# New planner numbers for the experts' stage: another order, another planned pitch of indirect transfers, three experts allowed to make low halves on TensorE and ScalarE

## The chip, the cores and the metric

The kernel runs on one core of a Trainium2 chip. The metric is the device time of one execution in microseconds (us), as the median of several runs; smaller is better. TensorE is called PE in the profile, its weight loads PEld, VectorE DVE, ScalarE ACT, GpSimd POOL and SyncE SP.

## The reference, cut to what matters

Three blocks follow each other: a linear attention with a delta rule, a dense block with a rational activation, and a block of eight experts to which every token is assigned once.

```python
def _moe2_ref(x, w_gate, w1, w2):          # x 3072 x 384, 8 experts, hidden 1024
    cap = N // E                           # 384 tokens for each expert
    logits = x @ w_gate
    order = np.argsort(-logits.flatten())  # best (token, expert) pairs first
    for idx in order:
        tok, e = (int(idx) // E, int(idx) % E)
        if assigned[tok] >= 0 or counts[e] >= cap: continue
        assigned[tok] = e; counts[e] += 1
    for e in range(E):
        mask = assigned == e
        out[mask] = np.maximum(x[mask] @ w1[e], 0.0) @ w2[e]
```

## The kernel before, in words

The attention and the dense block fill the first 609 us or so; the change does not touch them. The last stage, `tail`, does the eight experts. In each of its rounds one expert fills up (`Route.phase`: VectorE compares keys, TensorE counts with tiny matmuls into `rp`, six rounds of it one after another), which tells the number of the expert whose weights are to be loaded (`ix`) and its 384 tokens (`perm`, three columns of 128 row numbers).

For an expert n the work is this:

- `load` (line 782): two indirect transfers from GpSimd's queue bring `w1f` and `w2f`; `split` makes of each of 16 blocks a half-precision high part on ScalarE (line 793) and the low rest on VectorE (line 794). The parts lie in rings of two, named `w1s`/`w2s` or `wo` in the trace.
- `gather` (line 799): three indirect transfers bring 128 token rows each into `xg`.
- `transp`: TensorE transposes (line 816), ScalarE and VectorE write high and low parts `xe` (lines 819, 820).
- `up`: 8 blocks of 9 matmuls of 384 columns into `eph`, a ring of four (line 828). ScalarE writes the high half of the relu (line 831). The low half has two forms: VectorE computes it in one instruction (line 833), or TensorE subtracts the high half with a matmul by `neg` in the same bank (line 832) and ScalarE writes the relu of what is left (line 834).
- `down`: 3 tiles of 24 matmuls of 384 columns into `px` (line 841), ScalarE to `yo` (line 843), an indirect transfer to the output rows (line 846).

Nothing of this order is written by hand. `Sched` is a list scheduler that runs while the program is built: each piece of work has an engine (or a choice of engines), an assumed duration, the pieces it depends on, a priority (smaller is more urgent) and a latency after its end. At each step it takes the piece that can start first, and among equals the more urgent one. The pieces are then emitted in the order of their planned starts, and each engine works through its own list in that order on the chip, waiting where a semaphore isn't there yet. So the planned durations and the priorities set the order in every queue, GpSimd's of indirect transfers among them, and nothing else.

`PR` holds the priorities of the stage, for each kind of work eight numbers, one for each expert: `cz`, `hu` and `pm` for the routing, `px` transposes, `ev` high halves, `rs` low halves, `up` and `dn` matmuls, `sp`, `sq` and `sl` the weight split, `ga` gathers, `ld` loads, `sc` and `de` the output, `lt` the last matmuls of the dense block. `rp` says for which experts the form on TensorE and ScalarE may be chosen for the low half:

```python
g.add(('ACT',.42,lambda ...: activation(r[:,0,f],P,AF.Relu,scale=1.0-2.0**-11)),[Pn],[(rn,0,f)],pe)
k=g.add(([('PE',.169,lambda ...: matmul(P,s.neg,r[:,0,f],...))] if PR['rp'][n] else [])+
    [('DVE',.484,lambda ...: scalar_tensor_tensor(r[:,1,f],P,0.0,r[:,0,f],op0=OP.max,op1=OP.subtract))],...,ps)
g.add([('ACT',.371,lambda ...: activation(r[:,1,f],P,AF.Relu),lambda on,k=k: on[k]=='PE'),('NOP',0.0,None,...)],...,ps)
```

Of the kernel before, what the change touches and what calls it, by code (L numbers as in the profile page):

```python
# [22 lines left out]
class Att:  # L23
# [149 lines left out]
    def subst(s,m,eng,n16=False,D=None):  # L173
# [17 lines left out]
        if n16: load(None); z.append(lambda: nc.gpsimd.memset(x['W'],0.0))  # L191
# [326 lines left out]
class Ring:  # L518
# [1 line left out]
    def new(s): s.i+=1; return s.cur()  # L520
    def cur(s,d=0): k=(s.i-d)%len(s.t); return s.t[k],(s.name,k)

PR=dict(cz=[-8460.22,-3349.02,-1040.92,-4662.57,2286.09,-4542.55,-2851.07,-2830.4],
    hu=[-1158.71,2769.58,-1952.33,1420.35,20.61,-5092.86,1294.98,-2930.25],
    pm=[-827.35,-3434.29,-7199.64,-301.76,-9380.25,-789.5,-2507.28,-3094.98],
    px=[2213.47,-717.87,711.27,1083.3,-50.99,-1678.84,-176.44,-42.49],
    ev=[-2031.38,3896.44,-445.84,4974.79,-456.6,1410.8,-187.26,-280.73],
    rs=[3995.53,-838.36,3724.15,-2030.4,-5106.28,-2002.19,4963.77,-277.67],
    up=[1432.01,7925.78,415.8,19527.06,1302.29,-2496,-1028.3,393.52],
    dn=[-416.52,-263.26,2914.53,2346.47,7002.88,3039.18,1234.23,2541.59],  # L530
    sp=[-1250.53,-1034.63,-3233.17,3355.56,-2061.84,10814.9,2205.04,145.63],
    sq=[1182.66,5658.8,2518.53,1693.88,5502.59,2521.4,11976.42,-493.54],
    ga=[-91.9,220.07,-1393.31,1453.88,1738,-498.56,-1773.97,252.48],
    ld=[-763.16,-1461.53,2155.57,-1535.71,-2478.81,4661.21,334.89,-1356.37],
    sc=[1792.56,3025.86,-3657.49,-269.42,-11268.81,2802.89,972.48,366.12],
    de=[868.62,405.65,-1417.99,2091.14,378.47,2357.24,-3935.23,-63.01],
    rp=[1,0,0,0,0,0,0,0],
    sl=[9.7,-3928.78,-7440.7,1542.96,-6870.28,-1220,4305.31,-2018.78],
    lt=3989.8,
    tol=0.3)  # L540
class Route:

# [40 lines left out]
    def late(s,ctx): pass  # L583
# [178 lines left out]
class Experts:  # L762
# [16 lines left out]
    def load(s,n,ixn,late=[]):  # L779
        g=s.g; nc=s.nc; ix,ixd=ixn; a,an=s.w1f.new(); b,bn=s.w2f.new()  # L780
        fa=[(an,q) for q in range(8)]; fb=[(bn,q) for q in range(8)]; P1=PR['ld'][n]
        def ld(t,w,sh): return lambda: nc.gpsimd.indirect_dma_start(out=t.rearrange(sh),out_offset=None,in_=w,in_offset=bass.IndirectOffsetOnAxis(ap=ix,axis=0))  # L782
        g.add(('POOL',1.038,ld(a,s.w1,"p g j q -> p (g j q)")),[ixd],fa,P1,post=0.7); g.add(('DMA',4.4,None),fa,fa,0,post=0.9)
        g.add(('POOL',1.038,ld(b,s.w2,"p j f -> p (j f)")),[ixd]+late,fb,P1,post=0.7); g.add(('DMA',4.4,None),fb,fb,0,post=0.9)
        W1,W1n=s.w1s.new(); W2,W2n=s.w2s.new(); s.st.setdefault(n,{}).update(W1=(W1,W1n),W2=(W2,W2n))
        for q in range(16):
            if q<8: x=a[:,q]; W,Wn=W1,W1n; sc=W1S; xn=(an,q)
            else: x=b[:,q-8]; W,Wn=W2,W2n; sc=W2S; xn=(bn,q-8)
            s.split(n,q,x,xn,W[:,0,q%8],W[:,1,q%8],(Wn,0,q%8),(Wn,1,q%8),sc)
    def split(s,n,q,x,xn,h,l,hn,ln,sc):  # L790

        g=s.g; nc=s.nc; p=PR['sp'][n]+PR['sq'][n]*q
        g.add(('ACT',.43,lambda: nc.scalar.activation(h,x,AF.Copy,scale=sc)),[xn],[hn],p)
        g.add(('DVE',.484,lambda: nc.vector.scalar_tensor_tensor(l,x,sc,h,op0=OP.mult,op1=OP.subtract)),[xn,hn],[ln],p+PR['sl'][n])  # L794
    def gather(s,n,pmn):
        g=s.g; nc=s.nc; pm,pmd=pmn; s.st.setdefault(n,{})['pm']=pmn; s.st[n]['x']=s.xe.new()
        for i in range(3):
            t,tn=s.xg.new(); s.st[n]['g',i]=t,tn
            g.add(('POOL',1.038,lambda t=t,i=i: nc.gpsimd.indirect_dma_start(out=t,out_offset=None,in_=s.x2d,in_offset=bass.IndirectOffsetOnAxis(ap=pm[:,i:i+1],axis=0))),[pmd,'x2d'],[tn],PR['ga'][n],post=0.7)  # L799
            g.add(('DMA',.55,None),[tn],[tn],0,post=1.0)  # L800
    def late(s,M,T):

# [9 lines left out]
    def transp(s,n,i):  # L812
        g=s.g; nc=s.nc; xe,xn=s.st[n]['x']; t,tn=s.st[n]['g',i]; sl=slice(128*i,128*i+128); P,Pn=s.ph.new(); P=P.rearrange("p (j t) -> p j t",j=3); p=PR['px'][n]
        gv=t.rearrange("t (p j) -> t j p",j=3)
        def tr():
            for c in range(3): nc.tensor.transpose(P[:,c],gv[:,c],s.ident)  # L816
        k=g.add(('PE',.43,tr),[tn],[Pn],p)
        if (n,i)==(0,0): s.first=k
        g.add(('ACT',.44,lambda: nc.scalar.activation(xe[:,0,:,sl],P,AF.Copy,scale=X2S)),[Pn],[(xn,0,i)],p)  # L819
        g.add(('DVE',.5,lambda: nc.vector.scalar_tensor_tensor(xe[:,1,:,sl],P,X2S,xe[:,0,:,sl],op0=OP.mult,op1=OP.subtract)),[Pn,(xn,0,i)],[(xn,1,i)],p)  # L820
# [14 lines left out]
    def down(s,n):  # L835
        g=s.g; nc=s.nc; W2,W2n=s.st[n]['W2']; pm,pmd=s.st[n]['pm']; r,rn=s.st[n]['r']; pd=PR['dn'][n]; pe=PR['de'][n]
        for i in range(3):
            P,Pn=s.py.new(); o,o_n=s.yo.new()
            for f in range(8):
                for part,(rh,wh) in enumerate(((0,0),(0,1),(1,0))):  # L840
                    g.add(('PE',.17,lambda P=P,rh=rh,wh=wh,f=f,part=part,i=i: nc.tensor.matmul(P,r[:,rh,f,128*i:128*i+128],W2[:,wh,f],start=(f,part)==(0,0),stop=(f,part)==(7,2))),  # L841
                        [(rn,rh,f),(W2n,wh,f)],[Pn],pd+i)
            g.add(('ACT',.42,lambda P=P,o=o: nc.scalar.activation(o,P,AF.Copy,scale=1.0/(X2S*W1S*W2S))),[Pn],[o_n],pe)  # L843
            def out(o=o,i=i):
                nc.gpsimd.memset(s.sp,0.0)
                d=nc.gpsimd.indirect_dma_start(out=s.out,out_offset=bass.IndirectOffsetOnAxis(ap=pm[:,i:i+1],axis=0),in_=o,in_offset=None)  # L846
                for q in s.scat: s.tc.declare_no_dep(d.ins,q.ins,reason="rows of other tokens")
                s.scat.append(d)
            g.add(('POOL',1.08,out),[o_n,pmd],[('sc',o_n)],PR['sc'][n],post=0.7)
            g.add(('DMA',.55,None),[('sc',o_n)],[o_n,('sc',o_n)],0,post=1.0)  # L850
LG=1
def tail(R,X,M,T):
    g=R.g=X.g=Sched(); g.tol=PR['tol']; X.late(M,T)
    R.hurry=PR['hu'][0]; R.cz=PR['cz'][0]; R.pmk=PR['pm'][0]; L={0:R.phase(True)}
    def gather(n): X.gather(n,R.perm(L[n][0],PR['pm'][n]))
    def work(n):
        for i in range(3): X.transp(n,i)
        if n: X.down(n-1)
# [12 lines left out]

def units(g,M,T,u0,xT,newP,NP,O):
# [79 lines left out]
    rs=[-404.57,3136.8,145.19,-3450.88,-1193.48,50.75,4595.25,-486.29,7213.39,-1830.63,672.55,1692.55,767.94,149.92,-4898.99,-833.53],  # L952
    sq=[-4042.56,-4165.8,-3288.62,-1554.54,1129.42,1762.72,-228.16,-1123.11,690.54,4253.9,2705.63,-1743.23,-1487.85,-2504.2,2696.66,553.85],
# [88 lines left out]
class Banks:  # L1042
# [14 lines left out]
    q=[-46.86,-1341.62,713.15,-1006.91,-1360.96],  # L1057
# [50 lines left out]
    rs=-11545.17,  # L1108
    sq=-8925.36,
# [14 lines left out]
    q=1125.43,  # L1124
# [495 lines left out]
```

## Time and profile before

| what | value |
|---|---|
| median of 3 runs | 866.54 us (863.96 to 866.63) |
| the profiled execution's own time | 867.04 us |
| its span, first to last instruction | 865.3 us |
| PE, DVE, ACT, POOL busy | 93%, 85%, 65%, 48% of the span |
| mean granted clock of TensorE | 0.979 of full speed |

The profiled execution lies 0.5 us above the median of the runs. A busy share tells when an engine had an instruction under way; matmuls overlap in the trace, so that a stretch with one matmul after another shows each as about 0.33 us long although a new one starts twice as often. Idle time before an instruction is put down to what released it last.

### The profile page before, as it was taken

The numbers are of one execution on the slowest core, as the hardware profiler recorded it, in microseconds if no ns is written. First come the engines' busy times: TensorE is split into PE (matmuls) and PEld (weight loads), VectorE is DVE, ScalarE is ACT, GpSimd is POOL, SyncE is SP. The second block draws the span as 40 slices with busy tenths as digits, with TensorE's granted clock in tenths as the row PEclk, the third lists the DMA queues.
The fourth block names the chain that finished last, engine by engine and source line by source line (L and its number), as shares of the span: only waits on it lengthen the run. The fifth ranks groups of instructions, "written<-read, shape, count | busy, mean of one in ns | idle before, by whom it ended". The sixth has DMA issues, their size and how long they took to land. (4 is left out here: it accounts for less than half of the span.)

```text
span 865.3 us, 29590 instructions
## 1 busy us (share of the span) xinstructions
PE 808.9 (93%) x12536; PEld 581.0 (67%) x12536; DVE 739.5 (85%) x1696; ACT 563.8 (65%) x1039; POOL 416.8 (48%) x620
## 2 busy tenths in 40 slices
PE   8999789998999999999999999999899899999896
PEld 5887566776677767777777777766556556556563
DVE  8977987888889998998999999996889899889820
ACT  4236767888698787988888889881272451545520
POOL 2256820888678567865786232631221322242501
PEclk9999889999999999999999999999999999999999
DMA  9943387813532524251322201000450542355401
GB/s 362 280 137 84 103 203 211 248 62 75 116 85 81 107 83 97 82 108 31 87 75 67 42 21 39 19 2 20 146 220 29 191 184 112 109 201 229 155 11 45
DMA packets 89588, 98.62 MB, mean 114 GB/s; under 512 B 65776, under 2 KB 73584, under 8 KB 86640
## 3 DMA queue, kind: packets, MB, share of 16 engines
q1 hardware_dynamic: 83072, 59.31, 26.2%
q0 software_dynamic: 6096, 37.23, 11.7%
q8 instruction: 98, 1.61, 0.8%
q14 instruction: 34, 0.28, 0.1%
q10 hardware_dynamic: 288, 0.20, 0.1%
HBM read 74.43 MB, written 17.30 MB: 106 GB/s over the span
## 5 line engine op out<-in xcount | busy, mean ns | idle before, releaser
L936 PEld LDWEIGHTS <-wi 128*128 128x128 f16 x1728 | 168.6, 99 | 38.1 <-issue 6.3
L882 PE MATMUL px<-wo,gg 128*128 128x392 f16 (+1 forms) x1056 | 193.5, 330 | 0.0
L882 PEld LDWEIGHTS <-gg 128*128 128x128 f16 x1056 | 97.8, 98 | 61.8 <-issue 0.7
L900 POOL TENSOR_TENSOR gg<-w,gg 128x512 f16<-128x512 f32 x61 | 71.1, 1166 | 99.6 <-ACT gg L899 92.7
L936 PE MATMUL half<-xT,wi 128*128 128x256 f16 x864 | 107.1, 280 | 3.7 <-DVE wo L1320 2.5
L936 PE MATMUL ph<-xT,wi 128*128 128x256 f16 x864 | 104.2, 275 | 4.5 <-DVE w L913 2.3
L206 POOL TENSOR_TENSOR pmW<-pmW,pmT 128x31 f32<-128x31 f32 (+15 forms) x155 | 89.7, 579 | 10.8
L205 POOL TENSOR_TENSOR pmT<-pmW,pmA 128x31 f32<-128x31 f32 (+15 forms) x155 | 81.3, 525 | 10.9
L841 PEld LDWEIGHTS <-rr 128*128 128x128 f16 x576 | 52.1, 97 | 34.7 <-ACT rr L831 2.8
L846 POOL DMA_INDIRECT out_dram<-yo,perm x24 | 24.3, 1013 | 100.9 <-ACT yo L843 95.5
L831 ACT ACTIVATE rr<-eph 128x384 f16<-128x384 f32 x64 | 30.8, 488 | 59.5 <-PE eph L828 54.4
L899 ACT ACTIVATE gg<-w 128x512 f16<-128x512 f32 x88 | 55.4, 629 | 7.2 <-DVE w L913 6.7
L926 ACT ACTIVATE q<-q 128x512 f32<-128x512 f32 x88 | 54.8, 628 | 4.6 <-DVE q L925 4.5
L841 PE MATMUL px<-wo,rr 128*128 128x384 f16 x288 | 52.7, 330 | 2.4 <-ACT rr L831 2.3
L828 PE MATMUL eph<-xe,w1s 128*128 128x384 f16 x288 | 51.7, 333 | 1.5 <-ACT xe L819 1.0
L841 PE MATMUL px<-w2s,rr 128*128 128x384 f16 x288 | 52.9, 325 | 0.2 <-DVE w2s L794 0.2
L828 PE MATMUL eph<-xe,wo 128*128 128x384 f16 x288 | 51.7, 325 | 0.4 <-ACT xe L819 0.4
L799 POOL DMA_INDIRECT xg<-x2d,perm x24 | 26.4, 1100 | 46.9 <-issue 14.7
L1525 PE MATMUL px<-warm 128*128 128x256 f16 x344 | 44.6, 285 | 2.4 <-DVE warm L1505 2.4
L843 ACT ACTIVATE yo<-px 128x384 f32<-128x384 f32 x24 | 11.5, 490 | 44.9 <-PE px L841 35.7
L828 PEld LDWEIGHTS <-w1s 128*128 128x128 f16 x288 | 26.9, 99 | 19.7 <-issue 3.6
L925 DVE SCALAR_TENSOR_TENSOR q<-q,cf,ph 128x512 f32<-128x512 f32 x44 | 32.4, 737 | 8.7 <-ACT q L919 5.8
(398 smaller groups left out, 1897.6 us busy)
## 6 DMA issues: line engine op xcount, KB each, us to landing
kt<-in_k_dram SPq DMA_DIRECT2D x20, 512.0 KB, 4.5
kn<-in_k_dram SPq DMA_DIRECT2D x12, 384.0 KB, 4.7
qt<-in_q_dram SPq DMA_DIRECT2D x24, 192.0 KB, 3.8
vn<-in_v_dram SPq DMA_DIRECT2D x12, 384.0 KB, 4.4
x2d<-xr SPq DMA_DIRECT2D x44, 96.0 KB, 2.2
xT<-xs SPq DMA_DIRECT2D x22, 144.0 KB, 2.7
wsi<-in_moe_w_in_dram SPq DMA_DIRECT2D x3, 1024.0 KB, 5.4
wst<-in_moe_w_out_dram SPq DMA_DIRECT2D x8, 384.0 KB, 6.2
```

Of the source, the lines that this page charges most:

```text
L205: if half==0: eng.tensor_tensor(t,W[:,0:r,j:j+1].to_broadcast([n,r,k]),A[:,j:j+1,j+1:32].to_broadcast([n,r,k]),op=OP.mult)
L206: else: eng.tensor_tensor(W[:,0:r,j+1:32],W[:,0:r,j+1:32],t,op=OP.subtract)
L828: g.add(('PE',.169,lambda P=P,wh=wh,xh=xh,j=j,f=f,part=part: nc.tensor.matmul(P,W1[:,wh,f,j],xe[:,xh,j],start=(part,j)==(0,0),stop=(part,j ...
L831: g.add(('ACT',.42,lambda P=P,f=f: nc.scalar.activation(r[:,0,f],P,AF.Relu,scale=1.0-2.0**-11)),[Pn],[(rn,0,f)],pe)
L841: g.add(('PE',.17,lambda P=P,rh=rh,wh=wh,f=f,part=part,i=i: nc.tensor.matmul(P,r[:,rh,f,128*i:128*i+128],W2[:,wh,f],start=(f,part)==(0,0), ...
L882: te.matmul(T['px',un//8][bp][:,0:O.N],gg()[:,gh,i,128*bp:128*bp+128],M.wo[:,wh,fb,0:O.N],start=fb==0 and n==0,stop=fb==15 and n==2,skip_g ...
L899: ac.activation(T['gg',un][:,0].rearrange("p f t -> p (f t)")[:,a:b],T['w',un][:,a:b],AF.Copy)
L900: def gl(e): return lambda: e.tensor_tensor(T['gg',un][:,1].rearrange("p f t -> p (f t)")[:,a:b],T['w',un][:,a:b],T['gg',un][:,0].rearrang ...
L925: add(('DVE',.07+.6*z,lambda: ve.scalar_tensor_tensor(q(),q(),cf[:,4:5],P(),op0=OP.add,op1=OP.mult)),Q+Pn,Q,un+O.pd('mu',un))
L926: add(('ACT',.22+.37*z,lambda: ac.activation(q(),q(),AF.Abs)),Q,Q,un+O.pd('f2',un))
L936: for wh,xh in ((0,0),(0,1),(1,0)): te.matmul(T['P',un][:,i],M.wi[:,wh,part,128*fb:128*fb+128],xT()[:,xh,part],start=n==0,stop=n==8); n+=1
L1525: for _ in range(n): nc.tensor.matmul(bk[t or 'px1'][:,0:256],warm[:,0:128],warm,start=True,stop=True)
```

## The change

All of it is in numbers that the planner uses. Every priority of `PR` gets a new value; `rp` goes from one expert to three; an indirect transfer is planned with 1.27 us of GpSimd's time in place of 1.038 us (loads, gathers) or 1.08 us (outputs). No instruction's form, no tile and no other planned duration changes.

```diff
-PR=dict(cz=[-8460.22,-3349.02,-1040.92,-4662.57,2286.09,-4542.55,-2851.07,-2830.4],
...
-    lt=3989.8,
+PR=dict(cz=[-7021.72,-4284.48,1384.12,-7207.49,1083,-12767.81,-1178.86,-1110.34],
...
+    up=[496.03,1660.13,3217.1,3239.03,-324.52,-123.65,-619.57,-4288.44],
+    dn=[1561.31,5887.23,19537.55,-1015.14,85.3,922.9,1565.23,2415.17],
...
-    rp=[1,0,0,0,0,0,0,0],
+    rp=[1,1,1,0,0,0,0,0],
...
+    lt=-4685.38,
...
-        g.add(('POOL',1.038,ld(a,s.w1,"p g j q -> p (g j q)")),[ixd],fa,P1,post=0.7); g.add(('DMA',4.4,None),fa,fa,0,post=0.9)
-        g.add(('POOL',1.038,ld(b,s.w2,"p j f -> p (j f)")),[ixd]+late,fb,P1,post=0.7); g.add(('DMA',4.4,None),fb,fb,0,post=0.9)
+        g.add(('POOL',1.27,ld(a,s.w1,"p g j q -> p (g j q)")),[ixd],fa,P1,post=0.7); g.add(('DMA',4.4,None),fa,fa,0,post=0.9)
+        g.add(('POOL',1.27,ld(b,s.w2,"p j f -> p (j f)")),[ixd]+late,fb,P1,post=0.7); g.add(('DMA',4.4,None),fb,fb,0,post=0.9)
...
-            g.add(('POOL',1.038,lambda t=t,i=i: nc.gpsimd.indirect_dma_start(out=t,out_offset=None,in_=s.x2d,...
+            g.add(('POOL',1.27,lambda t=t,i=i: nc.gpsimd.indirect_dma_start(out=t,out_offset=None,in_=s.x2d,...
...
-            g.add(('POOL',1.08,out),[o_n,pmd],[('sc',o_n)],PR['sc'][n],post=0.7)
+            g.add(('POOL',1.27,out),[o_n,pmd],[('sc',o_n)],PR['sc'][n],post=0.7)
```

## Rows read from the trace of the kernel before

**Rows 1.** Windows: us, busy us and instructions of each engine, PEclk, DMA share, GB/s
```profile
623.50:857.00 233.50, 218.78 (x1676) 134.54 (x1676) 183.66 (x656) 104.01 (x239) 66.04 (x83) 0.99 0.38 140
660.00:745.00 85.00, 77.75 (x631) 48.05 (x630) 76.75 (x289) 36.64 (x85) 24.14 (x30) 0.99 0.41 149
742.70:746.10 3.40, 3.38 (x19) 1.79 (x17) 1.09 (x4) 2.13 (x5) 1.08 (x2) 0.50 0.09 37
```

**Rows 2.** Timeline of TensorE, two stretches: start, us, line, tiles, count, idle before
```profile
785.85 6.17 PE L828 MATMUL eph<-xe,wo 128*128 128x384 f16 x37
...
806.47 0.62 PE L816 MATMUL eph<-ident,xg 128*128 128x128 f32 x3 [1.36 <-DMA xg<-x2d,perm]
...
835.81 9.43 PE L841 MATMUL px<-w2s,rr 128*128 128x384 f16 x57
845.07 11.86 PE L841 MATMUL px<-wo,rr 128*128 128x384 f16 x72
```

**Rows 3.** Waits of TensorE from 623.5 to 857 us: us, times, longest
```profile
PE eph L816 <- DMA xg<-x2d,perm: 5.4, 8, 1.4
PE px L841 <- ACT rr L831: 2.3, 1, 2.3
PE rp L686 <- DVE fl L685: 2.2, 4, 1.2
PE eph L828 <- ACT xe L819: 1.5, 2, 1.0
```

**Rows 4.** Timeline of GpSimd's queue around two gathers: start, us, transfer, idle before
```profile
669.28 0.99 POOL L799 DMA_INDIRECT xg<-x2d,perm  x1 [7.42 <-issue]
670.58 0.96 POOL L799 DMA_INDIRECT xg<-x2d,perm  x1 [0.30 <-issue]
671.84 0.95 POOL L799 DMA_INDIRECT xg<-x2d,perm  x1 [0.30 <-PE rp L675]
673.09 1.18 POOL L782 DMA_INDIRECT w1f<-in_moe_w_dram,ix  x1 [0.30 <-DVE y L690]
674.58 1.20 POOL L782 DMA_INDIRECT w2f<-in_moe_w_dram,ix  x1 [0.31 <-issue]
...
801.38 3.03 POOL L799 DMA_INDIRECT xg<-x2d,perm  x1 [0.30 <-PE rp L751]
804.71 0.94 POOL L782 DMA_INDIRECT w2f<-in_moe_w_dram,ix  x1 [0.30 <-issue]
```

**Rows 5.** The gathers' tile: durations in ns, then us from issue to landing
```profile
L799 POOL DMA_INDIRECT xg<-x2d,perm x24: 945/990/3027, 619.8 to 812.2; - x24
...
DMA to landing us min/median/max: 3.0/3.5/5.7
```

**Rows 6.** Timelines of ScalarE and TensorE at one late weight load
```profile
680.38 1.35 ACT L793 ACTIVATE w1s<-w1f 128x384 f16<-128x384 f32 x3 [3.04 <-DMA w1f<-in_moe_w_dram,ix]
681.64 0.85 ACT L831 ACTIVATE rr<-eph 128x384 f16<-128x384 f32 x2
682.16 0.82 PE L841 MATMUL px<-wo,rr 128*128 128x384 f16 x4 [2.33 <-ACT rr L831]
```

**Rows 7.** Groups by line: xcount | busy, mean ns | idle before, releaser
```profile
L833 DVE SCALAR_TENSOR_TENSOR rr<-eph,rr 128x384 f16<-128x384 f32 x56 | 30.4, 551 | 9.6 <-ACT rr L831 9.5
L832 PE MATMUL eph<-rr,neg 128*128 128x384 f16 x8 | 1.9, 325 | 0.3 <-ACT rr L831 0.3
L834 ACT ACTIVATE rr<-eph 128x384 f16<-128x384 f32 x8 | 3.3, 500 | 0.0
```

**Rows 8.** Waits of TensorE from 660 to 745 us
```profile
PE rp L675 <- DVE cs L677: 1.4, 3, 0.9
PE rp L686 <- DVE fl L685: 0.7, 2, 0.4
PE eph L816 <- DVE rr L833: 0.5, 1, 0.5
PE rp L751 <- DVE pD L749: 0.4, 1, 0.4
```

**Rows 9.** Timeline of VectorE beside the long gather
```profile
801.17 2.42 DVE L794 SCALAR_TENSOR_TENSOR wo<-w1f,wo 128x384 f16<-128x384 f32 x5
```

**Rows 10.** Waits of ScalarE from 590 us on
```profile
ACT w1s L793 <- DMA w1f<-in_moe_w_dram,ix: 13.9, 4, 7.9
```

More of the change, by code (lines that the diff above doesn't have):

```diff
@@ L521, in cur @@
     def cur(s,d=0): k=(s.i-d)%len(s.t); return s.t[k],(s.name,k)
-PR=dict(cz=[-8460.22,-3349.02,-1040.92,-4662.57,2286.09,-4542.55,-2851.07,-2830.4],
[L524 to L536, printed above, removed]
-    rp=[1,0,0,0,0,0,0,0],
-    sl=[9.7,-3928.78,-7440.7,1542.96,-6870.28,-1220,4305.31,-2018.78],
-    lt=3989.8,
@@ new lines @@
+PR=dict(cz=[-7021.72,-4284.48,1384.12,-7207.49,1083,-12767.81,-1178.86,-1110.34],
+    hu=[4367.29,-1095.31,-2497.75,1447.83,-2105.69,-7597.14,1027.7,-2629.82],
+    pm=[-3475.17,1722.28,1057.64,-2113.23,5840.09,-4513.16,-1490.95,-956.24],
+    px=[-137.6,-3474.66,1460.08,448.12,1024.11,-342.1,861.87,-2871.22],
+    ev=[160.92,-3120.26,116.8,2928.69,551.57,543.59,1506.35,3637.96],
+    rs=[-3504.24,-511.95,5358.35,-300.41,-11135.9,-901.21,-336.22,-1754.47],
+    up=[496.03,1660.13,3217.1,3239.03,-324.52,-123.65,-619.57,-4288.44],
+    dn=[1561.31,5887.23,19537.55,-1015.14,85.3,922.9,1565.23,2415.17],
+    sp=[5811.28,5969.32,1234.8,-29.41,-1471.48,825.42,3800.92,4596.91],
+    sq=[681.16,5242.16,3332.63,25311.96,912.45,7313.85,33672.88,1654.22],
+    ga=[-724.27,-3968.76,5224.32,-173.49,3719.71,2350.61,-2575.84,-289.48],
+    ld=[6348.84,-1482.53,4524.46,-3311.1,3863.06,-2234.93,-1983.38,-1522.24],
+    sc=[-604.13,1497.92,-2905.62,6311.2,4227.11,-2931.29,-3523.47,3303.07],
+    de=[-35.98,1416.71,-8044.03,-6322.47,-7301,-4333.83,6190.61,1133.9],
+    rp=[1,1,1,0,0,0,0,0],
+    sl=[5589.05,2182.64,1906.44,223.23,932.54,496.68,3030.77,-666.54],
+    lt=-4685.38,
@@ L798, in gather @@
             t,tn=s.xg.new(); s.st[n]['g',i]=t,tn
-            g.add(('POOL',1.038,lambda t=t,i=i: nc.gpsimd.indirect_dma_start(out=t,out_offset=None,in_=s.x2d,in_offset=bass.IndirectOffsetOnAxis(ap=pm[:,i:i+1],axis=0))),[pmd,'x2d'],[tn],PR['ga'][n],post=0.7)
+            g.add(('POOL',1.27,lambda t=t,i=i: nc.gpsimd.indirect_dma_start(out=t,out_offset=None,in_=s.x2d,in_offset=bass.IndirectOffsetOnAxis(ap=pm[:,i:i+1],axis=0))),[pmd,'x2d'],[tn],PR['ga'][n],post=0.7)
             g.add(('DMA',.55,None),[tn],[tn],0,post=1.0)
```

## The prediction

> **What bounds the kernel now.** I read the windows first, because the change can act in the last stage alone. From the first transposition of gathered rows (623.5 us) to the last matmul (857 us) TensorE is busy for 218.8 of 233.5 us, VectorE for 183.7, ScalarE for 104.0 and GpSimd for 66.0 [rows 1]. TensorE sets the end: in its timeline the last 129 matmuls follow each other without a gap [rows 2], and what comes after 857 us is one output transfer and the end of the program, some 8 us that no order changes. A matmul of 384 columns costs (6.17 - 0.33)/36 = 0.162 us of this queue, not the 0.33 us of its record [rows 2]. So the time of the stage is TensorE's own work plus its idle time, 233.5 - 218.8 = 14.7 us. A new order can only win from those 14.7 us.
>
> The view of waits splits them: 5.4 us for gathered rows in 8 waits, 2.3 us in one wait for a high half, and smaller ones for the routing and the inputs on VectorE and ScalarE [rows 3]. VectorE is the second limit: between 660 and 745 us it is busy for 76.8 of 85 us, while TensorE idles for 85 - 77.75 = 7.25 us [rows 1]. GpSimd is far from full. Its transfers matter by the time at which they start.
>
> **The change part by part.** Every term is taken against the profiled execution's 867.04 us, which is 0.5 us above the median of the runs.
>
> *The pitch of transfers.* In GpSimd's timeline five transfers one behind the other start at 669.28 to 674.58 us, that is 1.33 us apart [rows 4], where the planner counted 1.038. The third gather thus starts 0.5 us later than planned and the load behind the gathers 3.81 - 3 x 1.038 = 0.7 us later. TensorE obeys its list and stands still at the transposition meanwhile. Eight waits of 5.4 us are 0.68 us each, about the size of this error. One of them, 1.36 us [rows 2], belongs to a gather that took 3.03 us instead of 0.99 [rows 4, 5], which no single planned number covers. Of the other 4.0 us I take two thirds as saved, 2.7 us: with 1.27 us the planner puts other matmuls ahead of the transposition. From issue to landing a gather takes 3.5 us [rows 5]; the plan's parts now add up to 1.27 + 0.7 + 0.55 + 1.0 = 3.52 us, before to 3.29. Bounds: nothing to 5.4 us saved.
>
> By the Trainium skill, page "SBUF — State Buffer", section "Who interferes with whom", a VectorE instruction with two inputs in SBUF shuts out a GpSimd instruction that reads SBUF until it is done. The trace agrees at one place: the gather of 3.03 us starts 0.21 us after the start of five weight splits, which run on VectorE for 2.42 us [rows 4, 9]. By the medians the sum below holds; by this rule it would be about 2.7 us higher, since no fixed pitch is right beside splits (a rival below).
>
> *The load behind the gathers.* At 680.38 us ScalarE has stood for 3.04 us before weights that haven't landed; behind it in its queue are two high halves, and for these TensorE waits 2.33 us [rows 6]. The load left 0.7 us late by the working above, so I take 0.7 us saved, bounds nothing to 2.3.
>
> *VectorE's relief.* At most 16 low halves (experts 1 and 2) leave VectorE. In a run each costs it (2.42 - 0.55)/4 = 0.47 us (2.42 us is the run of five splits, 0.55 the length of one record) [rows 7, 9], 7.5 us in all. Where they lie, between 660 and 745 us, TensorE waits for VectorE 1.4 + 0.7 + 0.5 + 0.4 = 3.0 us [rows 8]. I take half, 1.5 us. Bounds: nothing (the routing's chain sets those waits by its own length), 3.0 directly, and 7.5 if each routing round behind them moves forward whole.
>
> *What TensorE and ScalarE take over.* Sixteen matmuls by 0.162 us are 2.6 us on the engine that sets the end. The eight of expert 0 waited 0.3 us once for their high half [rows 7], so sixteen may add 0.6. Half of the 2.6 us should fall into the 7.25 us in which TensorE idles there anyway: cost 1.3 us, bounds nothing to 3.2; extra matmuls can't win time by themselves. A matmul by `neg` waits for ScalarE, and the next `up` matmuls stand behind it. ScalarE gets 16 x 0.50 = 8 us more [rows 7], which I price at nothing, covered by its 129 idle us of 233.5. That cover fails where the relu of a low half stands in ScalarE's queue behind a split whose weights aren't there: ScalarE waited 13.9 us in 4 such waits [rows 10]. Then the `down` matmuls that read the low half are late next, 2.3 us as in rows 6. If the planner finds VectorE free earlier it keeps the old form; then this term and the relief both vanish.
>
> *The clock.* From 742.7 to 746.1 us TensorE ran at a granted clock of 0.50, the lower level of 1.2 GHz [rows 1], just behind gather and routing waits. That costs about 1.7 us. If the waits shrink it may vanish; an order with other waits may have such a stretch elsewhere. I take 0.8 us saved, bounds 1.7 either way.
>
> *The order itself.* All priorities are new, so each queue (TensorE's, VectorE's, ScalarE's, GpSimd's transfers) is shuffled inside the rings. That moves no work off TensorE and is covered by the terms above. SP's queue and the first gather, at 619.8 us [rows 5], are not touched: it waits for rows of the dense block.
>
> Sum: 2.7 + 0.7 + 1.5 - 1.3 + 0.8 = 4.4 us less. 867.04 - 4.4 = 862.6, and with the 0.5 us to the median 862.1, say 862 us. All gains at their direct bounds and no cost give 12.4 us less, about 854; no gain, all costs (3.2), one late low half (2.3) and one more slow stretch (1.7) give 7.2 us more, about 874.
>
> **The rivals.**
> 1. *Low halves late on ScalarE (slower).* For experts 1 and 2 one relu each falls behind a split that waits for weights. Cost 2.6 + 0.6 + 2 x 2.3 = 7.8 us, against 2.7 + 0.7 from the pitch: 4.4 us more, about 871 us. For it: rows 6 and 10 show that very queue blocked. Against it: loads are planned later now, so splits are placed later too. It decides from the point where both experts have such a wait; with one it comes to 2.1 us more.
> 2. *The waits only change places.* TensorE idles for 14.7 us again behind other gathers and routing rounds, and the added matmuls hide in that or cost 1.3: 866.5 to 868 us. For it: a routing round is a chain between VectorE and TensorE [rows 8], whose length no order changes. Against it: 5.4 us of the waits have a cause that the new number removes.
> 3. *The relief passes on whole.* The routing behind experts 1 and 2 comes 7.5 us earlier instead of 1.5: 856 us. For it: VectorE at 90% there [rows 1]. Against it: TensorE would then have to find work for nearly all of its idle time.
> 4. *GpSimd held up by VectorE.* Two more gathers fall beside runs of splits and take 3 us, each with a wait of 1.36 us [rows 2]: 862.1 + 2.7 = 865 us. That is what the skill's page, named above, would lead to. For it: the one gather of rows 5. Against it: the median is 0.99.
>
> **How the numbers follow.** A measurement here tells about 0.3%, 2.6 us, from no change: faster is below 863.9 us, slower above 869.1. Chances: my forecast 0.42, rival 1 0.20, rival 2 0.17, rival 3 0.13, rival 4 0.08. Of my forecast's share 0.03 lies above 863.9. So faster 0.39 + 0.13 = 0.52, same 0.03 + 0.17 + 0.08 = 0.28, slower 0.20. The range of 855 to 870 us takes in all of my forecast, rivals 2 and 4, most of rival 3 and the lower half of rival 1; it leaves out about 0.15. The forecast's own range is 859 to 865 us, the terms at half or one and a half of their values.
>
> **What would show it.** The step on the pitch is right if TensorE's waits for gathered rows fall from 5.4 us to about 3 while GpSimd's pitch stays at 1.3 us. The relief is right if the instructions of line 832 rise from 8 towards 24, those of line 833 fall by as many, and the routing waits between 660 and 745 us halve. The wait at line 841 for a high half should shrink; if one of 2 us or more stands there for ScalarE's line 834, rival 1 is at work. Idle time of TensorE of 14.7 us as before, spread over other lines, is rival 2. A gather of over 2 us beside splits is rival 4. I am wrong as a whole if TensorE's idle time falls and the time does not, or if a stage before 609 us has moved.

## The result, and the profile after

The changed kernel takes 851.98 us, the median of 4 runs (848.24 to 854.94), against 865.25 (860.14 to 866.63) for the kernel before on the same chip: a ratio of 0.9855, with an interval of 0.9809 to 0.9901. The gain is about 13 us where the prediction had 4.4, and the time lies below the range of 855 to 870.

The profiled execution took 853.05 us, its span is 851.3. Not all of the difference of 14 us to the profiled execution before belongs to the change: line 1552, where the experts' stage is set up, starts at 589.71 us in the trace of before and at 587.35 in that of after, although the instructions ahead of it are in the same order on every engine. In the profiles of all kernels of this study, none of which changes this part, line 1552 starts at 585.1 to 593.3 us. From there to the first transposition it is 33.8 us before and 33.4 after. What follows is therefore told in the *stage*, from the start of the first transposition (line 816) to the end of the last matmul (line 841): 623.51 to 856.93 us before, **233.4 us**, and 620.70 to 842.96 after, **222.3 us**, that is 11.2 less. After it come 8.3 us in both (7.0 in the four runs below with transfers of SyncE, whose totals are shorter by these 1.3 us as well).

The windows after: us, busy us and instructions of PE, PEld, DVE, ACT and POOL, granted clock, DMA share, GB/s. The first is the stage, the second the stretch of [rows 1].

```profile
620.70:843.00 222.30, 216.89 (x1685) 134.28 (x1685) 179.48 (x647) 109.10 (x248) 67.28 (x83) 0.99 0.39 147
660.00:745.00 85.00, 82.71 (x717) 52.11 (x715) 79.40 (x320) 43.31 (x99) 27.06 (x33) 1.00 0.42 153
742.70:746.10 3.40, 3.40 (x23) 2.04 (x22) 3.40 (x18) 1.06 (x3) 2.67 (x4) 1.00 0.53 152
624.90:628.40 3.50, 3.50 (x23) 1.81 (x22) 1.97 (x10) 0.49 (x1) 0.00 (x0) 0.51 0.53 225
```

TensorE idles for 222.30 - 216.89 = 5.4 us by this view, 14.7 before, with nine matmuls more. Between 660 and 745 us it idles for 2.3 us instead of 7.25. The stretch of half clock at 742.7 us is gone; one early in the stage, which the kernel before has too, is left. TensorE is busy nearly all through such a stretch of 3.4 us at half the granted clock, so that one costs up to 1.7 us, an estimate from these windows.

The waits of TensorE in the stage, beside [rows 3] (us, times, longest); then from 660 to 745 us, beside [rows 8]:

```profile
PE eph L816 <- DMA xg<-x2d,perm: 3.3, 8, 0.8
PE rp L686 <- DVE fl L685: 0.6, 1, 0.6
PE eph L828 <- ACT xe L819: 0.6, 1, 0.6
PE rp L673 <- DVE ge L617: 0.4, 1, 0.4
PE px L841 <- ACT yo L843: 0.3, 1, 0.3
...
PE eph L816 <- DMA xg<-x2d,perm: 2.0, 4, 0.8
PE px L841 <- ACT yo L843: 0.3, 1, 0.3
```

The wait of 2.3 us for a high half has gone, and so have all waits for VectorE from 660 to 745 us. The gathers, and the groups of the low halves, beside [rows 5] and [rows 7]:

```profile
L799 POOL DMA_INDIRECT xg<-x2d,perm x24: 946/1132/1832, 616.4 to 798.7; - x24
...
DMA to landing us min/median/max: 3.0/3.2/3.8
...
L833 DVE SCALAR_TENSOR_TENSOR rr<-eph,rr 128x384 f16<-128x384 f32 x47 | 25.9, 552 | 8.5 <-ACT rr L831 8.3
L834 ACT ACTIVATE rr<-eph 128x384 f16<-128x384 f32 x17 | 8.0, 494 | 4.4 <-PE eph L832 4.4
L832 PE MATMUL eph<-rr,neg 128*128 128x384 f16 x17 | 5.2, 325 | 0.0
```

TensorE now makes 17 low halves, six for expert 0 and eleven for experts 1 and 2. GpSimd's pitch has not become shorter: from one gather's start to the next's it is 1.39 us by the median, 1.30 before. What changed is what stands around the gathers. GpSimd's timeline where the loads of expert 2 leave, beside [rows 4]:

```profile
663.41 0.99 POOL L782 DMA_INDIRECT w1f<-in_moe_w_dram,ix  x1 [6.47 <-DVE pn L715]
664.70 0.96 POOL L782 DMA_INDIRECT w2f<-in_moe_w_dram,ix  x1 [0.30 <-issue]
672.70 1.09 POOL L799 DMA_INDIRECT xg<-x2d,perm  x1 [7.04 <-PE rp L675]
674.09 1.13 POOL L799 DMA_INDIRECT xg<-x2d,perm  x1 [0.30 <-issue]
```

The loads leave 9.7 us earlier than in [rows 4], 6.9 if one counts from the start of the stage, ahead of the gathers instead of behind them.

### The profile page after: what moved, and what is told of

The parts are those of the page before. It is cut to its first block, busy times and chain, and to the rows that moved or that the text cites. A ratio compares the mean times of both kernels' runs of the same rounds, so it can differ in the third digit from the quotient of the medians.

```text
span 851.3 us, 29600 instructions
## 1 busy us (share of the span) xinstructions
PE 807.2 (95%) x12545; PEld 580.9 (68%) x12545; DVE 735.9 (86%) x1687; ACT 568.9 (67%) x1048; POOL 417.1 (49%) x620
## 3 DMA queue, kind: packets, MB, share of 16 engines
q0 software_dynamic: 6096, 37.23, 11.8%
## 4 chain that ended last, share of the span: by engine, by line
PE 52%; DVE 17%; issue 11%; DMA 7%; POOL 7%; ACT 3%; SPq 1%; POOLq 0%; DVEq 0%; ACTq 0%
PE px L882 13%; PE half L936 8%; PE ph L936 8%; PE eph L828 4%; PE px L841 3%; DMA xg<-x2d,perm 3%; POOL pmW L206 2%; PE px L1525 2%; POOL pmT L205 2%; PE tg L123 2%; PE tg L269 2%; PE px L761 1%; DVE w L913 1%; DMA w1f<-in_moe_w_dram,ix 1%; PE tg L260 1%
## 5 line engine op out<-in xcount | busy, mean ns | idle before, releaser
L846 POOL DMA_INDIRECT out_dram<-yo,perm x24 | 26.7, 1111 | 82.1 <-ACT yo L843 80.2
L1525 PEld LDWEIGHTS <-warm 128*128 128x128 f16 x352 | 33.8, 102 | 9.5 <-DVE warm L1505 2.4
```

The costliest lines, as they stand in the source:

```text
L1525: for _ in range(n): nc.tensor.matmul(bk[t or 'px1'][:,0:256],warm[:,0:128],warm,start=True,stop=True)
```

## The experiments

Each ran beside the kernel before on the same chip; the ratio is to that kernel. The stage comes from one profiled execution each, the ratio from several runs. *Old order* is the kernel before, *new order* the kernel after, with the edit named. A stage from one profile can be off by more than e1 shows: the stretches at half clock early in it last 3.4 us in the kernel after and 6.8 in e14, whose edit acts only later.

| run | edit | ratio, 95% interval | stage, us |
|---|---|---|---|
| before | | 1 | 233.4 |
| after | | 0.9855 [0.9809, 0.9901] | 222.3 |
| e1 | after once more | 0.9872 [0.9832, 0.9911] | 222.8 |
| e2 | old order, 2nd and 3rd gathers off GpSimd's queue | 0.9875 [0.9832, 0.9918] | 223.3 |
| e3 | new order, the same | 0.9818 [0.9781, 0.9856] | 217.3 |
| e4 | new order, 11 low halves back on VectorE | 0.9901 [0.9871, 0.9932] | 226.2 |
| e13 | new order, both | 0.9869 [0.9821, 0.9916] | 222.9 |
| e5 | old order, 16 low halves on TensorE | 1.0087 [1.0052, 1.0122] | 240.2 |
| e6 | old order, expert 2's loads first | 0.9984 [0.9961, 1.0007] | 230.9 |
| e15 | old order, e2 and e6 together | 0.9874 [0.9833, 0.9915] | 226.8 |
| e14 | new order, expert 2's loads last | 1.0067 [1.0039, 1.0095] | 239.2 |
| e16 | new order, e14 and e4 together | 1.0122 [1.0062, 1.0182] | 242.5 |
| e7 | old priorities, planned with 1.27 us | 1.0136 [1.0093, 1.0179] | 241.4 |
| e8 | old priorities, three experts allowed | 1.0049 [1.0027, 1.0072] | 234.7 |
| e9 | other priorities, planned with 1.40 us | 0.9947 [0.9919, 0.9975] | 225.8 |
| e10 | new order, gathers delayed | 0.9912 [0.9885, 0.9938] | 227.9 |
| e11 | e9, gathers delayed | 0.9928 [0.9905, 0.9952] | 229.0 |
| e12 | old order, gathers delayed | 1.0041 [1.0014, 1.0069] | 236.6 |

**e1: the kernel after once more.** No edit; it shows how far the stage repeats.

> The changed kernel once more, to see how well the time of the last stage repeats. By the two profiles that stage (first transposition of gathered rows to last matmul) took 233.4 us before and 222.3 us after, while the stages ahead of it, whose instructions are the same in both kernels, differed by 2.4 us. If the gain lies in the stage, this run shows 222 us there within 1.5 us, whatever the whole time does.

The stage repeats within 0.5 us, the ratio within its interval. Of the 13 us of the first measurement, 11 can be counted on.

**e2, e3: the second and third gather of each expert without GpSimd's queue.** SyncE brings as many bytes of fixed rows instead, so the assignment of tokens is left out for these rows. These transfers do not wait for the routing either: in e2 the two of expert 1 leave at 613.4 and 613.9 us, that expert's first gather at 637.4.

```diff
-lambda t=t,i=i: nc.gpsimd.indirect_dma_start(out=t, ... in_offset=IndirectOffsetOnAxis(ap=pm[:,i:i+1],axis=0))
+lambda t=t,i=i: nc.gpsimd.indirect_dma_start(... as before ...) if i==0 else nc.sync.dma_start(t,s.x2d[128*(3*n+i):128*(3*n+i)+128])
```

> The order of before, with the second and third gather of each expert as plain transfers of SyncE's queue (fixed rows, so which token goes to which expert is left out). That takes 16 transfers of 1.3 us from GpSimd's queue, and no transposition but an expert's first can wait for a late gather. Theory pitch (the old order was planned for gathers that come too soon, and in queues worked through in order each late one holds up other work behind it): the stage falls by 5 us or more, from 233.4 to about 228, with fewer waits on VectorE and ScalarE too. Theory order (the old order is simply worse, and gathers matter only where TensorE waits for them): it falls by about 3 us, the part of the 5.4 us of waits that the second and third gathers have, and the waits for routing steps and high halves stay.

> The same edit in the order of after (again the rows are fixed ones). Theory pitch: the new order already allows for late gathers, so the stage falls by 2 us or less from 222.3. Theory order: it falls like the old order did, by the second and third gathers' part of its 3.3 us of waits, about 2 to 3 us.

The stage falls by 10.1 us in the old order and by 5.0 in the new one. In e2 the theory of the pitch was right on the 5 us or more, but not on fewer waits for VectorE. In e3 both theories missed: 2 to 3 us was the most that either allowed. TensorE's waits in e2 from 620 us on:

```profile
PE eph L816 <- DMA xg<-x2d,perm: 2.3, 3, 1.3
PE rp L686 <- DVE fl L685: 2.2, 6, 0.8
PE rp L675 <- DVE cs L677: 1.7, 4, 1.0
```

Not all of the 10.1 us is shown to be the gathers', because the two stages ran at different clocks. The kernel before has two stretches at half clock in its stage (626.7 and 742.7 us), e2 none, and e3, e4 and e13 have the early one, like the kernel after. The early stretch before, the whole stage of e2, and the early stretches of e4, e13 and e3 (columns as above):

```profile
626.70:630.10 3.40, 3.40 (x17) 1.68 (x17) 1.74 (x7) 0.00 (x0) 0.00 (x0) 0.50 0.83 354
622.97:846.28 223.31, 214.09 (x1676) 133.27 (x1676) 183.49 (x656) 102.91 (x239) 50.47 (x68) 1.00 0.38 143
622.30:625.70 3.40, 3.32 (x21) 1.73 (x21) 1.56 (x5) 0.03 (x1) 0.00 (x0) 0.50 0.77 322
628.50:631.90 3.40, 3.18 (x21) 1.64 (x21) 1.71 (x5) 0.17 (x1) 0.00 (x0) 0.50 0.39 128
626.40:629.80 3.40, 3.08 (x20) 1.58 (x19) 1.80 (x5) 0.27 (x1) 0.00 (x0) 0.51 0.43 133
```

At 1.7 us for a stretch, 3.4 of the 10.1 us are clock, and 6.7 are left. Whether the gathers' waits bring the stretches on is open; e3 and e13 have the same fast gathers as e2 and still the early stretch. The listed wait for gathers fell by 5.4 - 2.3 = 3.1 us in the old order and by 3.3 - 0.8 = 2.5 in the new one, where the number of stretches is the same. So in both orders the stage fell by about twice what the line of waits lost, or more. The waits for VectorE stay: they are not the gathers' doing.

**e4: the low halves of experts 1 and 2 back on VectorE, in the new order**, at the places of the two instructions that they replace. It moves eleven, not the nine of which the expectation speaks.

```diff
-[('PE',.169,lambda ...: matmul(P,s.neg,r[:,0,f],start=False,stop=True))]
+[('PE',.169,(lambda ...: matmul(...)) if n==0 else None)]
-('ACT',.371,lambda ...: activation(r[:,1,f],P,AF.Relu), ...)
+('ACT',.371,(lambda ...: activation(...)) if n==0 else (lambda ...: nc.vector.scalar_tensor_tensor(r[:,1,f],P,0.0,r[:,0,f],op0=OP.max,op1=OP.subtract)), ...)
```

> The order of after, with the nine low halves of expert 1 that it gave to TensorE and ScalarE (17 less expert 0's eight) done by VectorE in the same places. VectorE gets 9 x 0.47 = 4.2 us more and TensorE 9 x 0.16 = 1.5 us less. Theory relief (the freed VectorE makes the gain): the stage takes 3 us or more longer, 225 us or above. Theories pitch and order: between 1.5 us shorter and 1 us longer.

The theory of the relief came true: it costs 226.15 - 222.26 = 3.9 us (3.4 against e1), with one early stretch at half clock in all three, although TensorE has eleven matmuls less, 11 x 0.162 = 1.8 us. VectorE's relief is thus worth 5.2 to 5.7 us gross. TensorE's waits in e4:

```profile
PE rp L673 <- DVE ge L617: 1.3, 1, 1.3
PE eph L828 <- DVE rr L834: 1.0, 1, 1.0
PE rp L739 <- DVE pc L738: 0.9, 1, 0.9
PE rp L710 <- DVE eo L701: 0.6, 1, 0.6
```

Four waits for VectorE that the kernel after does not have add up to 3.8 us, three of them on the routing. The group that VectorE got, with its xcount, busy us and mean ns:

```profile
L834 DVE SCALAR_TENSOR_TENSOR rr<-eph,rr 128x384 f16<-128x384 f32 x11 | 6.0, 549 | 0.0
```

**e13: both edits in the new order.**

```diff
+... if i==0 else nc.sync.dma_start(t,s.x2d[128*(3*n+i):128*(3*n+i)+128])   # gathers, as in e3
+('PE',.169,(lambda ...: matmul(...)) if n==0 else None)                    # low halves, as in e4
```

> The kernel after with two edits together: the second and third gathers of each expert are plain SyncE transfers of fixed rows (the assignment of tokens is left out for those rows), and the low halves of experts 1 to 7 that TensorE and ScalarE make are VectorE's again, at the same places. Alone the first gave a stage of 217.3 us, the second 226.2, the kernel after 222.3. Theory one (separate prices): the low halves cost their 3.7 us again, 220.5 to 221.5. Theory two (VectorE is late only because the gathers are): 217.5 to 218.8, their price is under 1.5.

With the gathers off the queue the low halves cost 222.93 - 217.31 = 5.6 us, more than the 3.9 with them on it and than theory one allowed. Theory two falls: VectorE was not late because the gathers were. And 222.9 is nearly the old order's 223.3: with fast gathers and the low halves on VectorE, the two orders are worth about the same, 0.4 us apart by the stages and 2.1 if the half-clock stretch of e13, which e2 lacks, is taken out. With the low halves on VectorE late gathers cost the new order only 226.15 - 222.93 = 3.2 us, for a line of waits that is 2.6 us shorter.

**e5: the low halves of experts 1 and 2 on TensorE in the old order**, at the places of VectorE's instruction.

```diff
-[('DVE',.484,lambda ...: scalar_tensor_tensor(r[:,1,f],P,0.0,r[:,0,f],op0=OP.max,op1=OP.subtract))]
+[('DVE',.484,(lambda ...: scalar_tensor_tensor(...)) if n not in (1,2) else (lambda P=P,f=f: [matmul(P,s.neg,r[:,0,f],start=False,stop=True),activation(r[:,1,f],P,AF.Relu)]))]
```

> The order of before, with the sixteen low halves of experts 1 and 2 done by TensorE and ScalarE in the places where VectorE did them. VectorE gets 16 x 0.47 = 7.5 us less, TensorE 16 x 0.162 = 2.6 us more. In the order of after the opposite edit on 11 low halves cost 3.6 us of the stage. Theory relief (VectorE's time alone counts): the stage falls by 3 to 5 us from 233.4. Theory pitch (in the old order late gathers set the pace, and VectorE only waits longer when it is freed): it changes by less than 1.5 us either way, or rises by up to 2.6.

Both theories missed: it is slower by 6.7 us of the stage. Of these, 16 x 0.162 = 2.6 us are matmuls, and 6.8 us more at half clock than before make up to 3.4. The ratio over eight executions says 7.5. The waits for routing steps do not get shorter: at lines 675, 686 and 751 TensorE waits 5.5 us for VectorE, 4.0 before. The exchange wins 3.9 us for eleven low halves where the order was made for it and loses 6.7 for sixteen where it was not. Here the matmul and the second relu stand where VectorE's instruction stood, which no planner chose; e8, in which the planner places them under the old priorities, gains nothing either.

**e6, e15: expert 2's loads ahead of its gathers, in the old order.** The planned starts of the `ix` step (line 706, third round) and of the two loads are moved 10 us ahead when the pieces are emitted; in e15 the edit of e2 is there too.

```diff
-for a0,_,f,i in sorted(order,key=lambda x:x[:2]): emit(a0,i,f)
+# key of a piece: its planned start plus s.sh.get(i,0), never below the keys of what it depends on
+for a0,o,f,i in sorted(order,key=lambda x:(key[x[3]],x[1])): emit(a0,i,f)
+g.sh.update({k:-10.0} if n==2 else {})   # at both transfers of load, and at the third ix step
```

> The order of before, with one thing moved: expert 2's index step on VectorE and its two weight loads go ahead of its three gathers, as in the order of after, where the loads left GpSimd 9.7 us sooner. All other queues keep their order. In the profile of before ScalarE stood 3.0 us for these weights and TensorE 2.3 us behind it. If that late load is a part of the gain, the wait of line 841 for a high half goes and the stage falls by 2 us or more; if the late gathers hold that stretch up anyway, less than 1 us, and the gathers of expert 2, now 2.7 us later in their queue, take the place of the wait.

> The kernel before with expert 2's loads ahead of its gathers and the second and third gathers of each expert as plain SyncE transfers of fixed rows (the assignment of tokens is left out for those rows). Alone the first gave a stage of 230.9 us, the second 223.3, the kernel before 233.4. Theory one (separate prices): 220.5 to 221.3. Theory two (the load was late only because it stood behind gathers, so that the two prices are one): 222.5 to 223.8.

In e6 the wait for a high half at line 841 shrinks from 2.3 us to none, and the stage is 2.5 us shorter. But its first transposition comes 1.2 us later behind its gather than before (4.9 us, 3.7 before). From the issue of that gather to the end of the stage the move wins 1.3 us, as much as the total says (0.9984 [0.9961, 1.0007], 1.4 us, not to be told from no change). One half-clock stretch fewer would be enough for that, and other waits open instead, 1.9 us at line 751 for VectorE (0.4 before).

For e15 stage and total disagree: the stage is 3.5 us longer than e2's, the total is e2's. Of the 3.5 us, 3.3 lie at one place, where a first gather takes 5.1 us from its issue to the transposition and a stretch at half clock follows. TensorE waits 2.17 us there, 0.61 in e2, and the stretch is worth up to 1.7:

```profile
793.80 0.81 PE L816 MATMUL eph<-ident,xg 128*128 128x128 f32 x3 [2.17 <-DMA xg<-x2d,perm]
...
794.00:797.40 3.40, 3.40 (x14) 2.26 (x14) 1.63 (x6) 0.98 (x2) 1.60 (x3) 0.51 0.89 355
```

Without these two e15 lies at 223.5 us, which is theory two: as far as one profile tells, the early loads win nothing where the gathers are off the queue. Prices that add up (220.5 to 221.3) do not fit the stage, and the total shows no sign of them.

**e14, e16: expert 2's loads behind its gathers, in the new order**, by the same means (loads 13.5 us later, and the splits behind them); e16 has the edit of e4 too.

```diff
+g.sh.update({k:13.5} if n==2 else {})   # at both transfers of load
```

> The kernel after with the two loads of expert 2 moved on GpSimd's queue from ahead of that expert's three gathers to behind them, as they stand in the kernel before; the splits of these weights follow later. Theory one (the load's place is worth in the new order what it was in the old): the stage goes from 222.3 to 224 to 225.5 and a wait for late splits of expert 2 at the second products comes back. Theory two (the new order has cover for it): under 1 us more.

> The kernel after with the loads of expert 2 behind its gathers and the low halves of experts 1 to 7 all on VectorE. Theory one (the prices are separate and the gathers' places in the order hold the rest): 228 to 229.5 us for the stage, so that some 4 to 5 of the 11 us are left between it and the kernel before. Theory two (low halves and load relieve the same waits): 226 to 227.5. If it comes to 232 or more, these two edits are the whole gain and the gathers' places none of it.

Both theories missed by far: the one edit costs 16.9 us, more than the whole gain. The timelines of GpSimd, ScalarE, VectorE and TensorE in e14 show one chain:

```profile
677.92 0.95 POOL L782 DMA_INDIRECT w1f<-in_moe_w_dram,ix  x1 [0.30 <-issue]
...
684.98 3.41 ACT L793 ACTIVATE w1s<-w1f 128x384 f16<-128x384 f32 x8 [11.42 <-DMA w1f<-in_moe_w_dram,ix]
...
685.53 3.37 DVE L794 SCALAR_TENSOR_TENSOR w1s<-w1f,w1s 128x384 f16<-128x384 f32 x7 [8.96 <-ACT w1s L793]
688.82 0.26 DVE L690 SCALAR_TENSOR_TENSOR y<-y,dd,dg 128x48 bf16<-128x48 bf16 x1
689.12 0.56 DVE L617 TENSOR_TENSOR ge<-y,ramp 128x768 bf16<-128x768 bf16 x1
...
689.73 0.34 PE L673 MATMUL rp<-oh,ge 128*128 128x32 bf16 x6 [11.77 <-DVE ge L617]
```

The load leaves at 677.92 us and ScalarE's split starts 7.1 us later. VectorE's half of the split waits for ScalarE's, and behind it in VectorE's queue stand the steps of the routing for which TensorE's next instruction waits. TensorE, with work for other experts further back in its queue, stands still for 11.8 us. The granted clock falls in this pause and stays low for the first microseconds of the work behind it; the windows of both (columns as above):

```profile
677.60:689.80 12.20, 0.43 (x5) 0.10 (x5) 4.24 (x10) 4.82 (x12) 1.99 (x4) 0.60 0.70 275
689.80:700.10 10.30, 10.30 (x77) 6.33 (x78) 8.45 (x41) 4.99 (x12) 3.05 (x3) 0.81 0.16 44
```

Of the 16.9 us, 11.8 are this one stop; an early stretch of 3.4 us more at half clock and the 3.9 us of half clock behind the stop make up to 3.7 more. With e14 as its base, e16 costs 3.3 us more, again about the price of the low halves. By the expectation of e16, 232 us or more would make the low halves and the load the whole gain. Its 242.5 us do not show that: they lie above the kernel before, so the late load does harm here that it does not do in the old order, and its price is no share of the gain.

**e7, e8: the two new permissions under the old priorities**, each alone, the order planned anew from them.

```diff
-('POOL',1.038, ...   # e7: both loads and the gather, and 1.08 for the output
+('POOL',1.27, ...
-rp=[1,0,0,0,0,0,0,0]  # e8
+rp=[1,1,1,0,0,0,0,0]
```

> The priorities of before, planned with 1.27 us for an indirect transfer, and nothing else. Theory pitch in its plain form (the measured number by itself makes the gain): the stage falls by 4 us or more. Theory search (the priorities are numbers found for one set of durations and mean little under another): the order changes in many places at once and the stage gets longer, 235 us or more, in spite of the truer number.

> The priorities and the pitch of before, with the form on TensorE and ScalarE allowed for three experts, and nothing else. The planner now chooses the form and the order around it moves too. Theory relief: the stage falls by 3 us or more from 233.4. Theory search: no gain, 232 us or more.

Both are slower than before. The theory of the search came true in both. In e7 the waits for gathers do fall, to 1.9 us, but others open. TensorE's waits from 620 us on:

```profile
PE rp L675 <- DVE cs L677: 4.6, 6, 1.3
PE rp L713 <- DVE gs L705: 3.6, 1, 3.6
PE px L841 <- ACT yo L843: 3.6, 3, 1.7
PE eph L816 <- DMA xg<-x2d,perm: 1.9, 3, 1.1
```

A truer number alone wins nothing here, under priorities found for another one.

**e9: other priorities, planned with a pitch of 1.40 us.** Only the numbers of `PR` and the four durations differ from the kernel after.

```diff
-('POOL',1.27, ...
+('POOL',1.4, ...
-PR=dict(cz=[-7021.72, ...],hu=[4367.29, ...], ...)
+PR=dict(cz=[-43976.15, ...],hu=[46543.09, ...], ...)
```

> The kernel after with other priorities for the steps of the expert stage, and with 1.40 in place of 1.27 us for each of the four transfers that GpSimd issues there (the median pitch of neighbours in the kernel after is 1.37 to 1.38 us); nothing else differs. Theory one, that an order pays when transfers come later than it reckoned with: the stage, 222.3 us in the kernel after, comes to 218 to 221 with less waiting for gathers than its 5.4 us, and the total is 0.2 to 0.6% below the kernel after's. Theory two, that the new order gains by its low halves and loads and the pitch is beside the point: any other order is as good or worse, 222 to 226 us.

The waits for gathers fell as expected, from 3.3 to 1.4 us (the line of the kernel after is 3.3, not the 5.4 that the expectation names), but the stage is 3.5 us longer, although it has no stretch at half clock. Other waits come instead, most of them for VectorE's steps. TensorE's waits in e9:

```profile
PE rp L686 <- DVE fl L685: 2.4, 5, 0.8
PE px L841 <- ACT yo L843: 1.9, 2, 1.6
PE rp L675 <- DVE cs L677: 1.8, 5, 0.8
PE eph L816 <- DMA xg<-x2d,perm: 1.4, 2, 1.1
```

VectorE's own group of low halves in e9 is late too (busy us, mean ns, then the idle time before them and what ended it):

```profile
L833 DVE SCALAR_TENSOR_TENSOR rr<-eph,rr 128x384 f16<-128x384 f32 x46 | 25.2, 554 | 15.0 <-ACT rr L831 14.8
```

VectorE stands for 14.8 us in front of low halves whose high halves ScalarE has not made (8.3 after). So it looks as if room for the gathers was bought with VectorE's order, which no run tests alone. Theory one holds for the gathers and fails for the stage, which lies in the range of theory two.

**e10, e11, e12: a memset of GpSimd ahead of each gather** (0.41 us each), in the new order, in that of e9 and in the old one.

```diff
-lambda t=t,i=i: nc.gpsimd.indirect_dma_start(...)
+lambda t=t,i=i: [nc.gpsimd.memset(s.sp,0.0),nc.gpsimd.indirect_dma_start(...)]   # s.sp is 1 x 384
```

> The kernel after with a GpSimd memset of 384 numbers on one partition ahead of each of its 24 gathers, so that neighbours come some 0.2 to 0.4 us further apart; the order is the same. Theory one (an order tolerates the pitch that it was made for and loses beyond it): the stage grows by 3 us or more, from 222.3 to 225 to 230, all of it in waits of the transpositions for gathers and in what these pass on. Theory two (the gathers' pitch is beside the point): it grows by less than 1 us.

> The order for 1.40 us with the same memset ahead of each gather. Theory one: it has some room left, so that it loses about half of what the kernel after loses by the same delay, 1 to 3 us. Theory two: the two lose alike, both next to nothing.

> The kernel before with the same memset ahead of each gather. Theory one: its order is already beyond the pitch of 1.04 to 1.08 us that it was made for, so each further 0.1 us comes out nearly in full: 5 us or more on the stage of 233.4 us, at least as much as the kernel after loses. Theory two: under 1 us.

The median start-to-start time of neighbouring gathers grew by 0.26 to 0.28 us in each (1.39 to 1.67 in the new order), so the third gather of each of eight experts comes 0.55 us later behind the first, 4.4 us in all. The stage of the new order lost 5.7 us (5.2 against e1), that of e9 3.2, the old one 3.1; by the totals it is 3.5 to 5, none (0.9928 after 0.9947), and 3.6. Of the 3.2 us, 1.7 can be a half-clock stretch that e9 lacks and e11 has, so what e9's order loses stays open. For the new and the old order the second theory, that this is beside the point, falls; but the old order does not lose more, as the first one had it. At the pitch that the chip has, the new order has no room left: more delay passes on nearly in full. It does not win by bearing lateness better from here on, it starts from a better place.

## Why the prediction was wrong

**The direction and the mechanisms named were right, but the low halves' net gain and the worth of the order were far too small.** Four stages, with and without the gathers on the queue, take the gain apart (in brackets the stretches at half clock in each):

| | gathers on GpSimd's queue | 2nd and 3rd off it (e2, e13, e3) |
|---|---|---|
| old order | 233.4 (2) | 223.3 (0) |
| new order, low halves of experts 1 and 2 on VectorE | 226.2 (1) (e4) | 222.9 (1) |
| new order, whole | 222.3 (1) | 217.3 (1) |

The low halves are worth 3.9 us with late gathers and 5.6 without. The order alone is worth 7.3 us where gathers are late and 0.4 where they are not. With each stretch taken out at 1.7 us, an estimate, this becomes 5.6 and 2.1. The ratios, whose executions carry the stretches as they happen to fall, say 0.0099 and 0.0006, that is 8.6 and 0.5 us, with intervals that allow for either reading. So most of the order's worth hangs on the gathers being on the queue, 3.5 to 6.9 us by the stages. The 11.2 us are then 5.6 for the order, 3.9 for the low halves and 1.7 for the clock, where the prediction had 3.4 (pitch and load), 0.2 and 0.8.

- **What bounds the kernel** held: TensorE sets the end, and the gain is its idle time, 14.7 us before and 5.4 after. The premise that only those 14.7 us can be won was loose. A record of 0.33 us at a pitch of 0.162 covers up to 0.16 us of a gap behind it; counted from start to start, with 0.162 us for a matmul of 384 columns, TensorE lost some 25 us of the stage before and about half of that after, of which 3.2 and 1.6 lie in the half-clock stretches. TensorE's busy time even fell by 218.78 - 216.89 = 1.9 us with nine matmuls more: the stretch that is gone had counted as busy.
- **The pitch of transfers, 2.7 us (bounds 0 to 5.4), with the order itself put at nothing beside it: a step that failed.** The listed waits for gathers fell from 5.4 to 3.3 us, about as said, and the pitch did not shrink. But the term took that line for all that late gathers cost, and it was 6.7 to 10.1 us in the old order (e2). Of what hangs on the gathers the new order saves 3.5 us, or 6.9 with the clock left in, against 2.7; only the second number is above the bound. Together with the load the order brought 5.6 us where 3.4 were forecast. The rest of a late gather's cost may lie in what stands behind a blocked transposition in TensorE's queue, and in gaps too short for the view; no run separates these.
- **The load behind the gathers, 0.7 us (bounds 0 to 2.3).** The wait of 2.3 us is gone. But the move alone wins 1.3 us in the old order (e6), and nothing that shows where the gathers leave the queue (e15), so it is no price of its own beside the gathers'. How much hangs on the place of these loads once the rest is packed tighter, 16.9 us in e14, no row of before showed.
- **VectorE's relief, 1.5 us, less 1.3 us for what TensorE and ScalarE take over: the step that failed by most, 0.2 net, measured 3.9.** Eleven low halves moved instead of 16, worth 11 x 0.47 = 5.2 us of VectorE by the prediction's price. Gross they won 5.2 to 5.7 us (3.4 to 3.9, and 1.8 for the matmuls). So the relief passed on whole, as rival 3 had it, where the prediction took half of the listed waits; the four waits of e4 for VectorE, 3.8 us, show where. The objection to rival 3, that TensorE would have to find work for nearly all of its idle time, was the wrong one: between 660 and 745 us it did, with 2.3 of 7.25 us left. But e5 and e8 show that this is no property of the exchange: in the old order it does not pay.
- **The clock, 0.8 us.** One of the two stretches at half clock in the stage is gone, 1.7 us, the upper bound. Part of that is luck: the prediction could not tell, and in other profiles the early stretch is absent (e2, e9, e15) or twice as long (e5, e8, e14, e16).
- **The sum.** 4.4 us was forecast for the total, 11.2 was measured on the stage. The prediction's own "all gains at their direct bounds and no cost", 12.4 us, is near to that by luck: its 7.7 us for pitch and load are more than the order's 5.6, its 3.0 for the low halves less than 3.9.
- **Rival 1** (low halves late on ScalarE) did not come: ScalarE waited 4.4 us in 9 places for TensorE's subtraction, and TensorE at line 841 for none of them. **Rival 2** (the waits change places) is what e7 and e9 do, not this change. **Rival 4**: no gather took over 2 us. The two longest, beside VectorE in the timelines of the two engines:

```profile
641.72 1.74 POOL L799 DMA_INDIRECT xg<-x2d,perm  x1 [10.09 <-DVE y L690]
787.13 1.83 POOL L799 DMA_INDIRECT xg<-x2d,perm  x1 [0.30 <-issue]
...
641.67 0.96 DVE L617 TENSOR_TENSOR ge<-y,ramp 128x1536 bf16<-128x1536 bf16 x1
787.13 1.02 DVE L794 SCALAR_TENSOR_TENSOR wo<-w1f,wo 128x384 f16<-128x384 f32 x2
```

Each starts with or just behind a VectorE instruction of two SBUF inputs and is longer than the shortest, 0.95 us, by 0.8 and 0.9, about the length of that work. The Trainium skill, page "SBUF — State Buffer", section "Who interferes with whom", says that such an instruction shuts GpSimd out until it is done; these two agree. The order of the starts matters: a gather at 694.78 us took 0.95 us although the same kind of `ge` instruction, 0.96 us long, started 0.08 us behind it. TensorE waited 0.63 us for the rows of the gather of 1.83 us, less than half of the 1.36 us that the prediction had for each.

What stays open: how much of the order's worth belongs to the gathers (3.5 to 6.9 us), what brings the half-clock stretches on, and why the new order's places carry the low halves so much better than the old ones; the runs show that they do.

## What to carry to other kernels

A late transfer can cost an in-order engine more than its line of waits says: here the stage won 5.0 us where the line lost 2.5, 6.7 to 10.1 where it lost 3.1, but only 3.2 where it lost 2.6. Price it by taking the transfer off its queue in one run, not by the wait alone, and compare the granted clocks of the two stages before you subtract them. Where a written order feeds several in-order queues, an edit is worth what the order around it makes of it (giving low halves to TensorE won 3.9 us in one order and cost 6.7 in another), so a corrected duration or a new choice of engine says little until the order is found anew.

## What was not expected of the hardware

- A memset of 0.41 us ahead of a gather on GpSimd moves the next gather by only 0.27 us: the idle time before a gather, 0.30 us at its neighbours, is 0.16 behind the memset.
- A pause of 11.8 us on TensorE was followed by half clock: 0.60 granted on average in the 12.2 us of the pause and 0.81 in the 10.3 us behind it. The same part of the kernel after runs at 1.00.
- Identical instructions ahead of the stage ended up to 8 us apart between profiles (585.1 to 593.3 us), while the stage itself repeated within 0.5 us in the one pair that there is. Early in the stage TensorE ran at half clock for 3.4 us in the kernel after and for 6.8 in e14, whose order is the same up to there.
